# A linear-attention layer and an MLP on one core, issued in an order that a list scheduler in the kernel works out

## The chip, the core and the metric

The kernel runs on one core of one Trainium2 chip. The core has five engines with an instruction queue each: PE (TensorE, matrix products), DVE (VectorE), ACT (ScalarE, also activation functions), POOL (GpSimd) and SP (SyncE, here only for DMAs). Each queue is worked off in its order; engines wait for each other through semaphores. Operands lie in SBUF, 128 partitions wide; PE writes to PSUM, which has eight banks of 512 fp32 columns. 16 DMA engines move data between HBM and SBUF, or within SBUF. The metric is the device time of one execution in microseconds (us), lower is better. A change of about 1% is what a measurement of this kernel can tell from none.

## What is computed

Attention over 8 batches, 8 heads, 576 tokens and head size 64 without a softmax, followed by an MLP on all 4608 tokens (512 → 2048 → 512) with h·cos(h) between its layers.

```python
def phi(x, c, s):
    r = np.maximum(x, 0.0)
    return np.concatenate([r * c, r * s], axis=-1)
q_p, k_p = phi(q, cos_w, sin_w), phi(k, cos_w, sin_w)    # by token: cos, sin of (pi/2) * pos / S
kv = np.einsum('bhsf,bhsd->bhfd', k_p, v)
z = np.sum(k_p, axis=2)
num = np.einsum('bhsf,bhfd->bhsd', q_p, kv)
den = np.einsum('bhsf,bhf->bhs', q_p, z)[..., None] + 1e-06
x = (num / den).transpose(0, 2, 1, 3).reshape(B * S, H * D)
h = x @ w_in
out = (h * np.cos(h)) @ w_out
```

## The kernel before

**Tiles.** A batch's 576 tokens are laid on 128 partitions in four full tiles of 128 tokens (t = 0 to 3) and half a tile (t = 4, 64 tokens). Two batches, an even and an odd one, use opposite halves of the partitions of t = 4, so that the half tiles of a pair make one full tile. All matrix operands are fp16, loads and outputs fp32.

**Stages of one batch.** `load` (L79) brings k, v and q into one raw buffer each (two DMAs on SP per tensor). `prep` (L89) computes relu(x)·cos and relu(x)·sin for a token tile: with `tensor_scalar` on DVE (L98), and in batch 0 the sine half on ACT (L96). `prep_v` (L102) casts v into the 65 columns of V1 (the last one is ones, for the denominator). `kv_group` (L111) makes 20 products of 65 columns for four heads (L117) and ACT copies the result into kvz (L120). `q_trans` (L123) transposes a tile of q, eight heads, on PE through an identity (L127) and ACT copies it to qT (L131). `num` (L136) makes eight products of 65 columns (L147; 16 for t = 4 of an odd batch), and DVE computes the denominator (L152), its reciprocal (L155) and x16 (L159). `x_trans` (L164) transposes x16 in four pieces on PE (L168), ACT copies it to xT (L176).

**Stages of the MLP.** `moe1` (L225) makes one bank of layer 1, four products of 512 columns (L230), and `gate` (L220) follows: the sine of h + pi/2 on ACT into ch (L222), the product with h on DVE into g (L223). 16 banks make a chunk, which is one batch's 512 main tokens. `moe1_rem` (L235) does the same for the 128 remaining tokens of a pair of batches, 64 products of 128 columns (L242). `moe2` (L257) makes 128 output rows with 16 products of 512 columns (L260); ACT copies them (L270, L280), SP stores them.

**Order.** `mlp(s)` (L285) lists the steps of layer 1 of batch s with the layer 2 of batch s − 1 spread in between; `attention(b)` (L178) lists the attention's steps; `spread` (L303) mixes the MLP of s with the attention of s + 1. The framework orders the engines' queues from there and sets all waits. PSUM is a pool of eight tiles of one bank each, given out in turn. Weights are loaded and cast to fp16 by DMAs on POOL: w_in (L330) after a small copy (L325) that waits for q of batch 0, w_out (L338) after one (L333) that waits for v of batch 1. The loads of batch 1 wait, through copies at L84, for the third quarter of w_in.

Of the kernel before, what the change touches and what calls it, by code (L numbers as in the profile page):

```python
# [13 lines left out]
F16 = mybir.dt.float16  # L14


@with_exitstack
def kernel(
# [21 lines left out]
    assert Dm == H * D and R == P // 2 and 2 * D == P  # L40


# [6 lines left out]
    for n in range(2):  # L49
# [7 lines left out]
    cpool = ctx.enter_context(tc.tile_pool(name="cpool", bufs=1))  # L57
    apool = ctx.enter_context(tc.tile_pool(name="apool", bufs=2))
    gpool = ctx.enter_context(tc.tile_pool(name="gpool", bufs=2))
    ppool = ctx.enter_context(  # L60
        tc.tile_pool(name="ppool", bufs=8, space=bass.MemoryType.PSUM))

    CS = cpool.tile([P, 2, 2, NT + 1], F32, name="CS")
    IDENT = cpool.tile([P, P], F16, name="IDENT")
    PIH = cpool.tile([P, 1], F32, name="PIH")
    w_in_sb = cpool.tile([P, NCT, Dff], F16, name="w_in_sb")
    w_out_sb = cpool.tile([P, NJT, Dm], F16, name="w_out_sb")
    V1 = [cpool.tile([P, NT + 1, H, D1], F16, name=f"V1_{n}") for n in range(2)]

    srcs = {"k": k, "v": v, "q": q}  # L70
    raw = {nm: cpool.tile([P, H, NT + 1, D], F32, name=f"{nm}m") for nm in srcs}
    kvzs, kps, qps, qts, xts, gts = {}, {}, {}, {}, {}, {}

    def tokens(ap, n):

        return (ap[..., 0:S5, :].rearrange("h (p t) d -> p h t d", t=NT + 1),
                ap[..., S5:S, :].rearrange("h (p t) d -> p h t d", t=NT))

    def load(b, name, after=None):  # L79
        if b >= B:  # L80
            return
        m, n = raw[name], b % 2
        if after is not None:
            nc.gpsimd.tensor_copy(out=m[0:2, 0, 0, 0:1], in_=after)  # L84
        five, four = tokens(srcs[name][b], n)
        nc.sync.dma_start(out=blocks(m, n), in_=five)
        nc.sync.dma_start(out=blocks(m, 1 - n)[:, :, 0:NT, :], in_=four)

    def prep(b, name, dst, t):  # L89


        in_ = raw[name][:, :, t, :]
        for g in range(2):
            sc = CS[:, b % 2, g, t:t + 1]
            if b == 0 and g == 1:
                nc.scalar.activation(out=dst[:, t, :, g, :], in_=in_, func=AF.Relu, scale=sc)  # L96
            else:
                nc.vector.tensor_scalar(  # L98
                    out=dst[:, t, :, g, :], in0=in_, scalar1=0.0, scalar2=sc,
                    op0=ALU.max, op1=ALU.mult)  # L100

    def prep_v(b):  # L102
        vt = raw["v"].rearrange("p h t d -> p t h d")
        for n, (t0, t1) in enumerate(((0, 2), (2, NT + 1)) if b == 0 else ((0, NT + 1),)):
            dst = V1[b % 2][:, t0:t1, :, 0:D]
            if b == 0 and n == 0:
                nc.scalar.activation(out=dst, in_=vt[:, t0:t1], func=AF.Copy)
            else:
                nc.vector.tensor_copy(out=dst, in_=vt[:, t0:t1])  # L109

    def kv_group(b, hb):  # L111
        kp, kvz = kps[b], kvzs[b]
        KV = ppool.tile([P, HB, D1], F32, name=f"KV{b}_{hb}", tag="ps")
        for hh in range(HB):
            h = hb * HB + hh
            for t in range(NT + 1):
                nc.tensor.matmul(  # L117
                    KV[:, hh, :], lhsT=kp[:, t, h].rearrange("p g d -> p (g d)"),
                    rhs=V1[b % 2][:, t, h, :], start=(t == 0), stop=(t == NT))
        nc.scalar.activation(  # L120
            out=kvz[:, hb * HB:(hb + 1) * HB, :], in_=KV, func=AF.Copy)

    def q_trans(b, t):  # L123
        src = qps[b][:, t]
        QP = ppool.tile([P, H, P], F16, name=f"QP{b}_{t}", tag="ps")
        for h in range(H):
            nc.tensor.matmul(  # L127
                QP[:, h, :], lhsT=src[:, h].rearrange("p g d -> p (g d)"),
                rhs=IDENT, is_transpose=True)
        qT = apool.tile([P, H, P], F16, name=f"qT{b}_{t}", tag=f"qT{t}")  # L130
        nc.scalar.activation(out=qT, in_=QP, func=AF.Copy)  # L131
        qts[(b, t)] = qT

    x16s = {}

    def num(b, t):  # L136

        parts = [(qts[(b, t)], kvzs[b])]
        if t == NT:
            parts.insert(0, (qts[(b - 1, t)], kvzs[b - 1]))  # L140
        N = [ppool.tile([P, HB, D1], F32, name=f"NUM{b}_{t}_{hb}", tag="ps")
             for hb in range(2)]
        for hb in range(2):
            for hh in range(HB):
                h = hb * HB + hh
                for n, (qT, kvz) in enumerate(parts):
                    nc.tensor.matmul(  # L147
                        N[hb][:, hh, :], lhsT=qT[:, h, :], rhs=kvz[:, h, :],
                        start=(n == 0), stop=(n == len(parts) - 1))
        den = apool.tile([P, H], F32, name=f"den{b}_{t}", tag="den")  # L150
        for hb in range(2):
            nc.vector.tensor_scalar_add(  # L152
                out=den[:, hb * HB:(hb + 1) * HB], in0=N[hb][:, :, D], scalar1=1e-6)
        rec = apool.tile([P, H], F32, name=f"rec{b}_{t}", tag="rec")
        nc.vector.reciprocal(out=rec, in_=den)  # L155
        x16 = apool.tile([P, H, D], F16, name=f"x16{b}_{t}", tag="x16", bufs=4)
        for hb in range(2):
            sl = slice(hb * HB, (hb + 1) * HB)
            nc.vector.tensor_tensor(  # L159
                out=x16[:, sl, :], in0=N[hb][:, :, 0:D],  # L160
                in1=rec[:, sl].unsqueeze(2).broadcast_to((P, HB, D)), op=ALU.mult)
        x16s[(b, t)] = x16

    def x_trans(b, t):  # L164
        x2 = x16s.pop((b, t)).rearrange("p h d -> p (h d)")
        XP = ppool.tile([P, NCT, P], F16, name=f"XP{b}_{t}", tag="ps")
        for c in range(NCT):
            nc.tensor.matmul(  # L168
                XP[:, c, :], lhsT=x2[:, c * P:(c + 1) * P], rhs=IDENT,
                is_transpose=True)  # L170
        if t < NT:
            dst = xts[b][:, :, t * P:(t + 1) * P]
        else:
            dst = xts[("r", b // 2)] = apool.tile(
                [P, NCT, P], F16, name=f"xTr{b}", tag="xTr")
        nc.scalar.activation(out=dst, in_=XP, func=AF.Copy)  # L176

    def attention(b, after=None):  # L178

        kps[b] = apool.tile([P, NT + 1, H, 2, D], F16, name=f"kp{b}", tag="kp", bufs=1)  # L180
        qps[b] = apool.tile([P, NT + 1, H, 2, D], F16, name=f"qp{b}", tag="qp", bufs=1)
        kvzs[b] = apool.tile([P, H, D1], F16, name=f"kvz{b}", tag="kvz", bufs=3)
        xts[b] = apool.tile([P, NCT, SM], F16, name=f"xT{b}", tag="xT")

        def pk(t):
            return lambda: prep(b, "k", kps[b], t)

        def pq(t):
            return lambda: prep(b, "q", qps[b], t)

        def ld(name):
            return lambda: load(b + 1, name, after)

        def of(f, t):
            return lambda: f(b, t)

        def pv():
            prep_v(b)
        if b == 0:
            steps = [pk(t) for t in range(NT + 1)] + [ld("k"), pq(0)]  # L200
            for t in range(1, NT + 1):
                steps += [of(q_trans, t - 1), pq(t)]
            steps += [ld("q"), of(q_trans, NT), pv, ld("v"), of(kv_group, 0),
                      of(kv_group, 1), of(num, 0)]
        else:
            steps = [pk(t) for t in range(NT + 1)] + [ld("k"), pv, ld("v")]
            steps += [of(kv_group, 0), pq(0), of(kv_group, 1), pq(1)]
            for t in range(2, NT + 1):
                steps += [of(q_trans, t - 2), pq(t)]
            steps += [ld("q"), of(q_trans, NT - 1), of(num, 0), of(q_trans, NT)]  # L210
        steps += [
                  of(num, 1), of(num, 2), of(x_trans, 0), of(num, 3),
                  of(x_trans, 1)]
        if b % 2 == 1:
            steps += [of(num, NT), of(x_trans, 2), of(x_trans, 3), of(x_trans, NT)]
        else:
            steps += [of(x_trans, 2), of(x_trans, 3)]
        return steps

    def gate(dst, M1, n):  # L220
        ch = apool.tile([P, SM], F32, name="ch", tag="ch", bufs=3)
        nc.scalar.activation(out=ch[:, 0:n], in_=M1, func=AF.Sin, bias=PIH, scale=1.0)  # L222
# [62 lines left out]
    def mlp(s):  # L285
# [8 lines left out]
        if not m1:  # L294
            return m2
# [76 lines left out]
```

## Time and profile before

| | |
|---|---|
| Median of three runs | 348.44 us (346.4 to 349.01) |
| The profiled execution's span | 347.7 us |
| PE / DVE / ACT busy | 308.7 / 213.2 / 185.9 us |
| HBM read, written | 36.74 MB, 9.44 MB |
| First layer-1 matmul | 30.65 us |
| Last matmul starts a group of 16 at | 339.24 us |
| k, q, v of batch 0: from first DMA issue to use | 0.74 to 7.15, 10.72, 14.08 us |
| Mean of one: gate on ACT, gate on DVE, prep on DVE, prep on ACT | 0.69, 0.69, 0.48, 0.63 us |
| Copy of a q transpose (1024), an x transpose (512), an output (512), all on ACT | 1.00, 0.60, 0.60 us |

How to read it: the page gives busy time by engine, then the span in 40 equal slices (each digit is the busy share in tenths, PEclk is the clock that TensorE was granted), the DMA queues, the chain of work that ended last, and the costliest groups of instructions. A group is named by line, engine, operation, and output <- inputs. The trace can also be asked for a timeline. Matmuls are pipelined: the duration of one in the profile includes its way through the array, so the pace is read from the starts.

### The profile page before, as it was taken

Reading aid. Unit: us, or ns where it says so; the run is one execution under the profiler, and the core shown is the slowest. Engines: PE = TensorE matmul, PEld = TensorE weight load, DVE = VectorE, ACT = ScalarE, POOL = GpSimd, SP = SyncE. Lnnn points to the kernel's source line nnn. Section 1 sums busy time; section 2 is a strip of 40 time slices with the busy share of each in tenths; the row PEclk is TensorE's granted clock in tenths of the full one; section 3 lists DMA queues with packets and bytes.
Section 4 is the critical chain, followed back from the end, with each engine's and each line's share of the span. In section 5 each row is a group of like instructions: output and inputs, shape, how many; then the busy total and the mean of one; then the engine's idle time right before and its main releaser. Section 6 shows DMA issues by size and latency. Waiting matters only on the chain.

```text
span 347.7 us, 6066 instructions
## 1 busy us (share of the span) xinstructions
PE 308.7 (89%) x2448; PEld 172.2 (50%) x2448; DVE 213.2 (61%) x486; ACT 185.9 (53%) x285; POOL 8.4 (2%) x19
## 2 busy tenths in 40 slices
PE   0555099599999999999999999999999999999994
PEld 0442066245565555455574555455655554446441
DVE  3536949978698499239983897356953481444100
ACT  1954048356755575356664665557555753555211
POOL 0400400000000000000000000000000000000000
PEclk9986679789999999999999999999999999999998
DMA  7999999226536464411833134301010010110121
GB/s 237 281 229 314 209 223 340 63 92 211 161 100 200 146 189 163 136 63 38 265 100 130 39 129 125 134 2 63 1 62 30 2 61 1 60 61 1 62 91 61
DMA packets 33084, 42.38 MB, mean 122 GB/s; under 512 B 1824, under 2 KB 30496, under 8 KB 33056
## 3 DMA queue, kind: packets, MB, share of 16 engines
q1 hardware_dynamic: 28544, 37.75, 32.9%
q0 software_dynamic: 4224, 4.19, 7.4%
q8 instruction: 19, 0.31, 0.4%
q14 instruction: 9, 0.07, 0.1%
q10 hardware_dynamic: 288, 0.04, 0.1%
HBM read 36.74 MB, written 9.44 MB: 133 GB/s over the span
## 4 chain that ended last, share of the span: by engine, by line
PE 81%; DVE 4%; issue 4%; ACT 3%; DMA 2%; POOL 0%; POOLq 0%; DVEq 0%
DMA km<-in_k_dram 2%; ACT ch L222 2%; DVE qp_332 L98 1%; PE M_4083 L260 1%; PE M_4044 L260 1%; PE M_3984 L260 1%; PE M_3876 L260 1%; PE M_3816 L260 1%; PE M_3757 L260 1%; PE M_3696 L260 1%; PE M_3421 L260 1%; PE M_2682 L260 1%; PE M_2424 L260 1%; PE M_2064 L260 1%; PE M_1780 L260 1%
## 5 line engine op out<-in xcount | busy, mean ns | idle before, releaser
L230 PEld LDWEIGHTS <-w_in_sb 128*128 128x128 f16 x512 | 48.0, 101 | 47.4 <-issue 7.4
L242 PEld LDWEIGHTS <-w_in_sb 128*128 128x128 f16 x256 | 14.8, 98 | 0.2
L127 PE MATMUL QP_0_115<-IDENT,qp_97 128*128 128x128 f16 x8 | 1.0, 311 | 12.9 <-ACT qp_97 L96 12.9
L109 DVE CAST V_1_73<-vm 128x2560 f16<-128x2560 f32 x4 | 11.3, 2814 | 0.0
L109 DVE CAST V_0_72<-vm 128x2560 f16<-128x2560 f32 (+1 forms) x4 | 10.2, 2539 | 1.4 <-DMA vm<-in_v_dram 1.4
L127 PEld LDWEIGHTS <-qp_97 128*128 128x128 f16 x40 | 4.2, 149 | 12.9 <-ACT qp_97 L96 12.9
L260 PEld LDWEIGHTS <-g_3716 128*128 128x128 f16 x64 | 6.3, 98 | 7.5
L260 PEld LDWEIGHTS <-g_3243 128*128 128x128 f16 x64 | 6.2, 98 | 7.3
L260 PEld LDWEIGHTS <-g_727 128*128 128x128 f16 x64 | 6.2, 98 | 7.1
L260 PEld LDWEIGHTS <-g_2729 128*128 128x128 f16 x64 | 6.2, 98 | 7.1
L260 PEld LDWEIGHTS <-g_1728 128*128 128x128 f16 x64 | 6.1, 97 | 7.1
L260 PEld LDWEIGHTS <-g_341 128*128 128x128 f16 x64 | 6.2, 98 | 7.1
L260 PEld LDWEIGHTS <-g_2242 128*128 128x128 f16 x64 | 6.1, 98 | 7.1
L260 PEld LDWEIGHTS <-g_1241 128*128 128x128 f16 x64 | 6.1, 98 | 7.1
L117 PE MATMUL KV_0_375<-V_1_73,kp_331 128*128 128x65 f16 x20 | 1.3, 243 | 8.7 <-DVE V_1_73 L109 8.7
L117 PEld LDWEIGHTS <-kp_331 128*128 128x128 f16 x40 | 2.5, 132 | 9.7 <-issue 9.5
L98 DVE TENSOR_SCALAR kp_331<-km,CS 128x512 f16<-128x512 f32 x10 | 4.2, 480 | 2.7 <-DMA km<-in_k_dram 2.7
L120 ACT ACTIVATE kvz_333<-KV_0_375 128x260 f16<-128x260 f32 x1 | 0.4, 388 | 9.3 <-PE KV_0_375 L117 9.3
L96 ACT ACT_TABLE_LOAD x1 | 1.3, 1283 | 7.1 <-DMA km<-in_k_dram 7.1
L98 DVE TENSOR_SCALAR kp_96<-km,CS 128x512 f16<-128x512 f32 x5 | 2.1, 480 | 4.7 <-DMA km<-in_k_dram 4.7
L223 DVE TENSOR_TENSOR g_3716<-M_3717,ch 128x512 f16<-128x512 f32 x1 | 0.7, 691 | 6.9 <-ACT ch L222 6.9
L223 DVE TENSOR_TENSOR g_1728<-M_1729,ch 128x512 f16<-128x512 f32 x1 | 0.7, 693 | 6.6 <-ACT ch L222 6.6
(1072 smaller groups left out, 841.4 us busy)
## 6 DMA issues: line engine op xcount, KB each, us to landing
out_dram<-ost SPq DMA_DIRECT2D x32, 256.0 KB, 2.4
km<-in_k_dram SPq DMA_DIRECT2D x8, 640.0 KB, 5.3
qm<-in_q_dram SPq DMA_DIRECT2D x8, 640.0 KB, 6.0
vm<-in_v_dram SPq DMA_DIRECT2D x8, 640.0 KB, 7.0
km<-in_k_dram SPq DMA_DIRECT2D x8, 512.0 KB, 4.9
qm<-in_q_dram SPq DMA_DIRECT2D x8, 512.0 KB, 4.8
vm<-in_v_dram SPq DMA_DIRECT2D x8, 512.0 KB, 7.3
w_in_sb<-in_moe_w_in_dram POOLq DMA_DIRECT2D x4, 512.0 KB, 9.1
```

The source lines that it names most:

```text
L96: nc.scalar.activation(out=dst[:, t, :, g, :], in_=in_, func=AF.Relu, scale=sc)
L98: nc.vector.tensor_scalar(out=dst[:, t, :, g, :], in0=in_, scalar1=0.0, scalar2=sc, op0=ALU.max, op1=ALU.mult)
L109: nc.vector.tensor_copy(out=dst, in_=vt[:, t0:t1])
L117: nc.tensor.matmul(KV[:, hh, :], lhsT=kp[:, t, h].rearrange("p g d -> p (g d)"), rhs=V1[b % 2][:, t, h, :], start=(t == 0), stop=(t == NT))
L120: nc.scalar.activation(out=kvz[:, hb * HB:(hb + 1) * HB, :], in_=KV, func=AF.Copy)
L127: nc.tensor.matmul(QP[:, h, :], lhsT=src[:, h].rearrange("p g d -> p (g d)"), rhs=IDENT, is_transpose=True)
L222: nc.scalar.activation(out=ch[:, 0:n], in_=M1, func=AF.Sin, bias=PIH, scale=1.0)
L223: nc.vector.tensor_tensor(out=dst, in0=M1, in1=ch[:, 0:n], op=ALU.mult)
L230: nc.tensor.matmul(M1, lhsT=w_in_sb[:, c, j * P:(j + 1) * P], rhs=xts[b][:, c, :], start=(c == 0), stop=(c == NCT - 1))
L242: nc.tensor.matmul(M1[:, jj, :], lhsT=w_in_sb[:, c, j * P:(j + 1) * P], rhs=xts[("r", pr)][:, c, :], start=(c == 0), stop=(c == NCT - 1))
L260: nc.tensor.matmul(M2, lhsT=gts[key][:, j, gsl], rhs=w_out_sb[:, j, :], start=(j == 0), stop=(j == NJT - 1))
```

## The change

The whole function is rewritten; what each stage computes stays. What differs:

- A class `Plan` collects steps, each with an engine, an assumed occupancy and latency, a due time, and what it reads and writes. `run` is a list scheduler: it gives each engine in turn the ready step that can start first, the earlier due time first, and returns all steps by their start. The steps are then issued in this order, and the framework's own ordering is off (`manual_schedule`); it still sets the waits.
- All buffers are allocated once. PSUM is four tiles of two banks: two for layer 1, one for layer 2, one (ATT) for attention.
- The remainders of the eight batches (8 x 64 = 512 tokens) are gathered in xR and run as a ninth chunk, after batch 7.
- Layer 1 of chunks 0 and 1 runs by token halves: two products groups of 256 columns fill a bank.
- From batch 2 on, q tiles and x tiles are transposed by DMAs on SP, within SBUF; the batch 1 remainder's x too. Batch 0 leaves out t = 4 of q until layer 1 has begun (`late_q0`).
- The cosine half of every prep is on DVE, the sine half on ACT (batch 0's t = 4 of q apart, both on DVE). V is cast by token tile, in batches 0 and 1 by head halves and on both engines.
- num's denominator and x16 are one DVE instruction each for all heads, not two.
- w_in waits for the first half of v of batch 0, w_out for the second quarter of w_in, the loads of batch 1 (but for v's second half) for the third quarter of w_out.
- ACT's sine table is loaded at the start by a tiny activation. The last output tile is copied in two halves, on ACT and DVE, and stored from two queues.

```diff
+class Plan:
+    LINK = {"PE": 0.12, "ACT": 0.05, "DVE": 0.05, "POOL": 0.1, "SP": 0.0}
...
+        while len(order) < len(st):
+            best = None
+            for e, cand in ready.items():
+                for n in cand:
+                    t = max(free[e], avail[n])
+                    key = (t, st[n]["due"], n)
+                    if best is None or key < best[0]:
+                        best = (key, e, n)
+            (t, _, _), e, n = best
...
+        return [st[n] for n in sorted(order, key=lambda n: (st[n]["start"], n))]
...
-    ppool = ctx.enter_context(
-        tc.tile_pool(name="ppool", bufs=8, space=bass.MemoryType.PSUM))
+    M1P = [ppool.tile([P, 2, SM], F32, name=f"M1_{n}") for n in range(2)]
+    M2P = ppool.tile([P, 2, Dm], F32, name="M2")
+    ATT = ppool.tile([P, 2, SM], F32, name="ATT")
+    M1 = [M1P[n // 2][:, n % 2, :] for n in range(4)]
+    M2 = [M2P[:, n, :] for n in range(2)]
...
+    MM, MMH, MMA, MMT = 0.2157, 0.109, 0.031, 0.057
+    T0, TW, TP = 17.0, 46.0, 30.0
+    start = [T0, TW] + [TW + 14.0 + TP * n for n in range(NC)]
...
+    def q_dma(b, t, due):
+        dst, dkey = qdst(b, t)
+        pl.add("SP", 0.62, 0, due, lambda: nc.sync.dma_start(
+            out=dst, in_=qp[:, t].rearrange("p h g d -> p (h g d)"), transpose=True),
+            [("qp", t, g, h) for g in range(2) for h in range(H)], [dkey],
+            dma=(262.0, 200.0))
...
+    def x_dma(b, t, n, due):
+        dst, dkey = xdst(b, t)
+        pl.add("SP", 0.62, 0, due, lambda: nc.sync.dma_start(
+            out=dst, in_=x16[n].rearrange("p h d -> p (h d)"), transpose=True),
+            [("x16", n)], [dkey], dma=(131.0, 200.0))
...
+    def gate(bank, key, dst, dkeys, due):
+        c = chn[0] % NCH
+        chn[0] += 1
+        act(0.59, due, lambda: nc.scalar.activation(
+            out=ch[c], in_=bank, func=AF.Sin, bias=PIH, scale=1.0), [key, "PIH"], [("ch", c)])
+        dve(0.61, due, lambda: nc.vector.tensor_tensor(
...
+    def layer1(c):
+        X = xT[c % 2] if c < B else xR
...
+        for j in range(NJT):
+            m = m1n[0] % 4
+            m1n[0] += 1
+            due = start[c] + j * width[c] / NJT
+            def mm(m=m, j=j):
+                for cc in range(NCT):
+                    nc.tensor.matmul(M1[m], lhsT=w_in_sb[:, cc, j * P:(j + 1) * P], rhs=X[:, cc, :],
+                                     start=(cc == 0), stop=(cc == NCT - 1))
+            pe(NCT, MM, due, mm, xk + [("w_in", j // 4)], [("M1", m)])
+            gate(M1[m], ("M1", m), G[:, j, :], [("g", c % 2, j, t) for t in range(NT)], due + 1.5)
...
+    def attention(b):
+        T = start[b]
...
+        early = b == 1
+        base = T - 37.0
+        for nm in "kqv":
+            if early:
+                hold_raw(nm, 2)
+            load(b, nm, base - 12, HALVES if early and nm == "v" else (slice(0, H),))
+        for t in range(NT + 1):
+            for g in range(2):
+                prep(b, "k", t, g, "DVE" if g == 0 else "ACT", base + 1.5 * t)
...
+            if early:
+                q_pe(b, t, *BANKS[t % 4], "ACT" if t % 2 else "DVE", tt + 1)
+            else:
+                q_dma(b, t, tt + 1)
...
+    with tc.manual_schedule():
+        setup()
+        for s in pl.run():
+            s["fn"]()
```

## The prediction

> **What bounds the kernel now.** I read the page's head and slices first, then the timeline of TensorE (PE) over the first 70 us, then a dense stretch.
>
> ```profile
> span 347.7 us, 6066 instructions
> PE 308.7 (89%) x2448; PEld 172.2 (50%) x2448; DVE 213.2 (61%) x486; ACT 185.9 (53%) x285; POOL 8.4 (2%) x19
> ...
> PE   0555099599999999999999999999999999999994
> ...
> PEclk9986679789999999999999999999999999999998
> DMA  7999999226536464411833134301010010110121
> ```
>
> PE is full from slice 8 on, and full of holes before (a slice is 8.7 us). The timeline shows the holes; its columns are start, length, engine, line, operation, count, and the idle time before with what ended it:
>
> ```profile
> 30.65 1.86 PE L230 MATMUL M_342<-xT_99,w_in_sb 128*128 128x512 f16 x4 [0.69 <-ACT xT_99 L176]
> 32.31 1.91 PE L230 MATMUL M_354<-xT_99,w_in_sb 128*128 128x512 f16 x4
> 34.02 1.49 PE L230 MATMUL M_365<-xT_99,w_in_sb 128*128 128x512 f16 x4
> 44.20 1.26 PE L117 MATMUL KV_0_375<-V_1_73,kp_331 128*128 128x65 f16 x20 [8.70 <-DVE V_1_73 L109]
> ...
> 66.74 0.40 PE L168 MATMUL XP_4_688<-IDENT,x_4_665 128*128 128x128 f16 x2 [3.77 <-DVE x_4_665 L159]
> ```
>
> The first layer 1 starts at 30.65, stops after three banks, and PE waits 8.7 us for batch 1's cast. From starts in dense stretches PE pushes a 512-column matmul in 0.216 us, 128 columns in 0.057, 65 columns in 0.031. Before: 512+576 of the first (234.7), 256+320+144 = 720 of the second (41.0), 640 of the third (19.8): 295.5 us of work. The last matmul is pushed at 342.7 (339.24 + 16 x 0.216). Up to 68.8 it had pushed 23.7 us of work (80 QP, 80 KV, 80 NUM, 36 XP, 56 layer-1 matmuls), so **45 us are lost before 68.8**; after it 273.9 us hold 271.8 of work. PE's work plus the start is the time; DVE and ACT are idle 40% and more, and 5.0 us follow the last push.
>
> [...] three groups from 30.65 take 1.71 us each instead of 0.86, PEclk 0.5 to 0.8. [...]
>
> **The change, part by part.**
>
> *PE's work.* 240 q transposes and 112 x transposes leave PE (352 x 0.057 = **−20.1**). Layer 1 keeps its columns: four remainders of 128 columns become a ninth chunk of 512, chunks 0 and 1 run 256 columns wide (0.108 each). After: 448+576 x 0.2157 + 256 x 0.108 + 112 x 0.057 + 640 x 0.031 = **274.7 us**.
>
> *Start.* The w_in hold on POOL moves from q to v's first half, so k, q and v (landed at 7.1, 10.7, 14.0) no longer share the wires with it until about 12.5; its first quarter then lands about 16 to 17, not late for layer 1. I follow the built order: ACT's sine table is loaded early (1.28 us out of the way); kp and qp to about 13; four transposes to 14.2; their copies (1.0 each, alternately DVE and ACT, on two-bank tiles) to 16.8, V's casts in between; KV's second half waits for ACT's copy of the first, 18.0; NUM about 19.3 to 20.2; x16 on DVE (0.15+0.2+0.75) 21.0 and 22.1; two xT copies by 23.4; layer 1 at **23.8** instead of 30.65, with 4.7 us of work pushed: 19.1 lost. Cold clock on it, as at 30.65 before: 2.5.
>
> *Batch 1.* w_out now loads during layer 1 of chunk 0, where before w_out waited for v of batch 1 (36.3); k, q and half of v of batch 1 are held for w_out's third quarter. 15.5 MB in all, at the 300 to 390 GB/s of the loads before, land by about 50; layer 2 of chunk 0 (13.8 us of work) covers that. At chunk 1's start NUM, x16, transpose and copy follow each other with little in between: three x16 in a row (0.75 each), two copies of 0.6, a fourth NUM and its chain: about **6** lost. Queued behind these waits are kp and qp of batch 2 on ACT and DVE, which wait for loads themselves; they gate xT's last copies, but at 62 to 66 us, about when PE gets there.
>
> *A new wait.* PSUM is now four tiles of two banks each, and the built order shows that the waits are by tile, not by bank. Where layer 1 runs alone, PE writes both banks; sine 1 waits for both, product 1 for it, sine 2 for product 1, product 2 for sine 2, and PE's next write into either bank for product 2. Durations:
>
> ```profile
> 149.90 1.03 PE L230 MATMUL M_1770<-xT_1236,w_in_sb 128*128 128x512 f16 x4
> 150.96 0.69 ACT L222 ACTIVATE ch<-M_1770,PIH 128x512 f32<-128x512 f32 x1 [0.18 <-PE M_1770 L230]
> 151.68 0.69 DVE L223 TENSOR_TENSOR g_1728<-M_1770,ch 128x512 f16<-128x512 f32 x1 [0.17 <-ACT ch L222]
> ```
>
> The group is pushed by 150.76, the sine starts 0.20 later. Chain: 0.20 + 4 x 0.69 + 4 hops (0.03 to 0.05) = 3.1 us, and 1.73 of writing: 4.83 us for every two pairs of banks, in which PE has 3.45 us to do. **1.4 lost for each four banks after the first four.** Chunks 0, 1 and 2 run all 16 banks so (3 x 1.4 each), chunk 3 about 13, chunk 4 about 10: 12.6 + 3 + 2.1 = about 18. Other instructions in the DVE and ACT queues between (preps 0.48 and 0.63, V's casts) add about 3.
>
> From there layer 1 and layer 2 alternate. There the second bank's write waits for sine 1: 0.20 + 0.69 + 0.05 = 0.94 against 0.86 of layer 2 in between, 35 x 0.08 = 2.8. Layer 2's two banks wait for each other's copy: 0.20 + 0.60 + 0.05 = 0.85 against 0.86, nothing while ACT is free; if it isn't, up to 0.6 each. NUM waits for DVE's x16 through one tile ATT, 1.5 us against 1.7 to 2 of cover: 3 in all. Preps in ACT's and DVE's queues: 3.
>
> *Work moved between DVE and ACT.* ACT gets about 70 preps (x 0.63) and loses 30 qT copies (1.0) and 28 xT copies (0.6); DVE loses the preps. Both stay near 60% busy: nothing, as long as the orders hold.
>
> *SP.* 30 q transposes (262 KB) and 28 x transposes (131 KB) go into SP's in-order queue, before later loads and stores. Per batch: 5 of the first, 4.5 of the second, 10 other DMAs at 0.63. [...] hidden, since each transpose stands some 10 us or more of PE work ahead of its reader. Bounds: at a load's rate 0.8 us; if the queue is held until landing, like the nearest rows (2.4 to 6.0 us), some 5 us. [...] Nothing on PE waits then.
>
> *Tail.* The last output is copied in two halves and sent from two queues: 4.3 instead of 5.0 us.
>
> **Sum:** 274.7 + 19.1 + 2.5 + 6 + 18 + 3 + 2.8 + 3 + 3 + 4.3 = 336.4 against the span of 347.7; the median of the runs is 0.7 above that span, so **337**.
>
> **Rivals.**
> - *The pair waits cost little* (0.17): sine, sine, product, product stands in places, which shortens the chain to 2.9 us, and idle time of DVE and ACT speaks for it. Without most of the 30 us of waits: about 316.
> - *SP becomes the bound* (0.20), slower than before: a q transpose that holds SP for 5 us makes a batch 25 + 11.3 + 6.3 = 42.6 us against a chunk's 33, over six batches +58: about 395. It decides from 3.7 us per q transpose ((33 − 6.3) / 7.25); at 4.2 it equals the time before. For it: every transpose stands before loads in one queue, and nothing here has measured one. Against: the later slices show DMA mostly at 0 to 4 tenths[...].
> - *The queues pile up* (0.13): loads of batches 2 and 3 stand in ACT's and DVE's order before work that PE waits for; each late load of 3 to 5 us stops all. Three or four of these: about 352.
> - *The fixed order doesn't do what it says*, PE keeps its holes: then the start stays at 45 lost, less 20 of work, plus the waits: in the pile-up case.
>
> **How the numbers follow.** The forecast's case has 0.50 and its own range is 322 to 346. Within 1% (345.0 to 351.9, about what a measurement of this kernel can tell from no change) lie a few hundredths of it and about half of the pile-up. Faster: 0.44 + 0.17 = 0.61; same 0.12; slower, from the SP case and the rest of the pile-up, 0.27. The range 317 to 372 leaves out about half of the first rival and most of the SP case's upper part.
>
> **What would show it.** Right: first layer-1 matmul near 24 us; in chunks 0 to 2 PE idle before each second pair, ended by DVE's product, about 1.1 and 0.3 us in turn; few waits on DMA transposes; PE pushing 274.7 us of work[...]. Wrong: PE waiting for xT or qT from SP, issues of 4 us and more, or PE near full from 24 us on.

## The result and the profile after

| | before | after |
|---|---|---|
| Median of four runs | 347.42 us (346.25 to 349.01) | 352.28 us (350.4 to 353.1) |
| The profiled execution's span | 347.7 us | 348.6 us (time 350.4) |
| First layer-1 matmul | 30.65 us | 23.59 us |
| PE's work by the pace of starts | 295.6 us | 274.7 us |
| Time PE lost from then to its last push | 22 us, to 342.7 us | 50 us, to 343.8 us |

In the trace of before a matmul of 512 columns lasts 379 ns and the next starts 216 ns after it, one of 128 columns lasts 219 ns at a pace of 57, one of 65 columns 193 ns at a pace of 31.

The ratio is 1.0125, 95% interval 1.0076 to 1.0175: the change made the kernel slower by 1.25%. The forecast was 337 us and faster. A single execution below, of the version with refitted times, took 867.75 us, as PE pushed most of its 512-column matmuls in 0.62 us in place of 0.216, and the ratio there leaves it out. The head and slices of the changed kernel's page:

```profile
span 348.6 us, 5319 instructions
...
PE 292.8 (84%) x2032; PEld 154.1 (44%) x2032; DVE 181.0 (52%) x387; ACT 179.2 (51%) x290; POOL 7.9 (2%) x19
...
PE   0478899676888779878988998999999999999983
...
PEclk9989999999999999999999999999999999999998
DMA  6999958999999989798494641561041010101111
```

PE begins earlier and has 20 us less to do, and all of it is lost again in sixes, sevens and eights that reach to slice 25, at an almost full clock (0.99 on average) and with DVE and ACT at 52% and 51%. The chain of work that ended last says who holds PE: 57% of it is PE, 19% ACT, 12% DVE. The view of PE's waits (who waited for whom: us in total, times, longest):

```profile
PE M L436 <- ACT ost L448: 10.9, 20, 0.9
PE M L412 <- DVE gT L370: 9.0, 14, 1.3
PE M L395 <- DVE gT L370: 6.5, 7, 2.0
```

L412 and L395 are layer 1, waiting for the gate's product. L436 is layer 2, waiting for the copy of a bank by ACT. The second and third were forecast as a loss; the first was named in the prediction and put at nothing. How they come about is seen in the timeline. In chunk 2, where layer 1 runs alone (start, length, engine, line, operation, count, idle before):

```profile
113.06 1.89 PE L412 MATMUL M<-xT,w_in_sb 128*128 128x512 f16 x8 [1.28 <-DVE gT L370]
...
113.64 0.69 ACT L368 ACTIVATE ch<-M,PIH 128x512 f32<-128x512 f32 x1 [0.78 <-DVE gT L370]
114.35 0.69 DVE L370 TENSOR_TENSOR gT<-M,ch 128x512 f16<-128x512 f32 x1 [0.75 <-ACT ch L368]
115.04 0.69 ACT L368 ACTIVATE ch<-M,PIH 128x512 f32<-128x512 f32 x1 [0.72 <-PE M L412]
115.10 1.89 PE L412 MATMUL M<-xT,w_in_sb 128*128 128x512 f16 x8 [0.16 <-DVE gT L370]
...
115.76 0.69 DVE L370 TENSOR_TENSOR gT<-M,ch 128x512 f16<-128x512 f32 x1 [0.71 <-ACT ch L368]
116.48 1.29 ACT L368 ACTIVATE ch<-M,PIH 128x512 f32<-128x512 f32 x2 [0.76 <-DVE gT L370]
```

Sine, product, sine, product follow each other without overlap, 0.70 us apart; PE writes the next pair (115.10) when the earlier pair's second product is over, and the one after that at 117.95. That is 4.89 us for four banks (113.06 to 117.95), as worked out in the prediction (4.83), for 3.45 us of work.

The tail of the program has layer 2 alone. PE, and what ACT does at the same time:

```profile
332.62 3.61 PE L436 MATMUL M<-w_out_sb,gT 128*128 128x512 f16 x16 [0.69 <-ACT ost L448]
336.92 3.61 PE L436 MATMUL M<-w_out_sb,gT 128*128 128x512 f16 x16 [0.69 <-ACT ost L448]
341.22 2.75 PE L436 MATMUL M<-w_out_sb,gT 128*128 128x512 f16 x12 [0.69 <-ACT ost L448]
```

```profile
331.98 0.60 ACT L448 ACTIVATE ost<-M 128x512 f32<-128x512 f32 x1 [3.70 <-PE M L436]
336.27 0.60 ACT L448 ACTIVATE ost<-M 128x512 f32<-128x512 f32 x1 [3.70 <-PE M L436]
```

ACT has been idle for 3.70 us, so the copy is as early as it can be; still PE, which goes on to the *other* bank, begins only when the copy is done. From 332.62 to 336.92 are 4.30 us, in which PE has 16 x 0.2157 = 3.45 us of work: **0.85 us lost per bank**, although ACT is free. In the kernel before, where each bank is a tile, the same stretch has no such gap: PE starts a bank every 3.45 us, and the copy of the bank before runs beside it.

```profile
332.34 3.62 PE L260 MATMUL M_4044<-w_out_sb,g_3716 128*128 128x512 f16 x16
332.54 0.60 ACT L270 ACTIVATE ost<-M_4025 128x512 f32<-128x512 f32 x1 [2.86 <-PE M_4025 L260]
335.79 3.62 PE L260 MATMUL M_4064<-w_out_sb,g_3716 128*128 128x512 f16 x16
```

Where layers 1 and 2 alternate, the copy stands behind a sine that the pair of layer 1 had delayed:

```profile
243.31 0.69 ACT L368 ACTIVATE ch<-M,PIH 128x512 f32<-128x512 f32 x1 [1.91 <-DVE gT L370]
243.90 0.59 ACT L448 ACTIVATE ost<-M 128x512 f32<-128x512 f32 x1
```

and PE's next write to layer 2's tile stands at 244.54, after an idle 0.50 us (it started the group before at 243.18 and pushed it in 0.86).

Adding up, over the whole trace, each matmul's start less the start and the push of the one before gives this comparison with the terms of the prediction's sum:

| Term | predicted | after |
|---|---|---|
| PE's work | 274.7 | 274.7 |
| Lost before the first layer-1 matmul | 19.1 | 18.9 |
| Cold clock on layer 1 | 2.5 | 0 |
| Chunk 1's start (42.9 to 67.7 us) | 6 | 4.2 |
| Layer 1 alone, pair waits and queued work | 18 + 3 | 22.9 |
| Layer 2's waits for copies | **0** | **14.3** |
| Alternation, num, preps | 2.8 + 3 + 3 | 8.5 |
| Tail | 4.3 | 4.8 |
| Span | 336.4 | 348.3 (348.6 in the trace) |

The 14.3 are 8.5 between one bank of layer 2 and the next (10 x 0.85) and 5.8 where layer 2 follows layer 1 (12 times).

### The profile page after: what moved, and what is told of

Same layout as the page of the kernel before. It is cut to its first block, busy times and chain, and to the rows that moved or that the text cites. A ratio compares the mean times of both kernels' runs of the same rounds, so it can differ in the third digit from the quotient of the medians.

```text
span 348.6 us, 5319 instructions
## 1 busy us (share of the span) xinstructions
PE 292.8 (84%) x2032; PEld 154.1 (44%) x2032; DVE 181.0 (52%) x387; ACT 179.2 (51%) x290; POOL 7.9 (2%) x19
## 3 DMA queue, kind: packets, MB, share of 16 engines
q1 hardware_dynamic: 75520, 49.17, 53.3%
## 4 chain that ended last, share of the span: by engine, by line
PE 57%; ACT 19%; DVE 12%; issue 6%; DMA 4%; SPq 0%; DVEq 0%; ACTq 0%
PE M L436 28%; PE M L412 20%; ACT ch L368 10%; DVE gT L370 10%; PE M L395 5%; DMA qm<-in_q_dram 4%; ACT ost L448 4%; ACT qp L233 2%; PE ATT L257 2%; PE ATT L319 1%; DVE x L329 1%; ACT V L246 1%; PE M L288 1%; ACT kp L233 1%; ACT qT L292 0%
## 5 line engine op out<-in xcount | busy, mean ns | idle before, releaser
L370 DVE TENSOR_TENSOR gT<-M,ch 128x512 f16<-128x512 f32 x144 | 98.2, 690 | 110.1 <-ACT ch L368 53.9
L368 ACT ACTIVATE ch<-M,PIH 128x512 f32<-128x512 f32 x144 | 96.6, 686 | 112.5 <-DVE gT L370 83.3
L436 PE MATMUL M<-w_out_sb,gT 128*128 128x512 f16 x576 | 141.0, 379 | 11.4 <-ACT ost L448 10.9
L412 PE MATMUL M<-xT,w_in_sb 128*128 128x512 f16 x384 | 94.7, 378 | 11.7 <-DVE gT L370 9.0
L436 PEld LDWEIGHTS <-gT 128*128 128x128 f16 x576 | 54.6, 97 | 76.7 <-issue 18.1
L412 PEld LDWEIGHTS <-w_in_sb 128*128 128x128 f16 x448 | 43.2, 97 | 68.2 <-issue 21.1
L395 PE MATMUL M<-xT,w_in_sb 128*128 128x256 f16 x256 | 30.4, 272 | 8.3 <-DVE gT L370 6.5
L448 ACT ACTIVATE ost<-M 128x512 f32<-128x512 f32 x35 | 20.6, 592 | 32.1 <-PE M L436 32.1
L395 PEld LDWEIGHTS <-w_in_sb 128*128 128x128 f16 x256 | 24.6, 97 | 13.1 <-issue 6.8
L233 ACT ACTIVATE kp<-km,CS 128x512 f16<-128x512 f32 x40 | 26.2, 712 | 4.9 <-DMA km<-in_k_dram 4.9
L233 ACT ACTIVATE qp<-qm,CS 128x512 f16<-128x512 f32 x39 | 26.2, 713 | 2.7 <-DMA qm<-in_q_dram 2.7
L329 DVE TENSOR_TENSOR x<-ATT,rec 128x512 f16<-128x512 f32 x30 | 20.6, 688 | 0.6
L412 PE MATMUL M<-xR,w_in_sb 128*128 128x512 f16 x64 | 16.4, 379 | 0.0
```

The lines of the kernel that those rows point to most:

```text
L233: act(0.2 + 0.37 * f, due, lambda: nc.scalar.activation(out=out_, in_=in_, func=AF.Relu, scale=sc), rd, wr)
L329: dve(0.62, due, lambda: nc.vector.tensor_tensor(out=x16[n].rearrange("p (b h) d -> p b h d", b=2), in0=N[:, :, :, 0:D], in1=rec[n].rearra ...
L368: act(0.59, due, lambda: nc.scalar.activation(out=ch[c], in_=bank, func=AF.Sin, bias=PIH, scale=1.0), [key, "PIH"], [("ch", c)])
L370: dve(0.61, due, lambda: nc.vector.tensor_tensor(out=dst, in0=bank if len(dst.shape) == 2 else bank.rearrange("p (j s) -> p j s", j=dst.sh ...
L395: nc.tensor.matmul(M1[m][:, jj * 2 * P:(jj + 1) * 2 * P], lhsT=w_in_sb[:, cc, j * P:(j + 1) * P], rhs=X[:, cc, ts], start=(cc == 0), stop= ...
L412: nc.tensor.matmul(M1[m], lhsT=w_in_sb[:, cc, j * P:(j + 1) * P], rhs=X[:, cc, :], start=(cc == 0), stop=(cc == NCT - 1))
```

## Experiments

Theory A: the waits go by PSUM tile, not by bank, so engines that use different banks of one tile follow each other in program order, in layer 1 and in layer 2. Theory B: the DMA transposes hold PE up, through late xT and qT or by their traffic. Theory C: the order that the list scheduler fixes is at fault, in whatever tiles. The kernel before ran beside all of them, 347.3 to 347.5 us; ratios are to it.

### Layer 1's and layer 2's banks as tiles of their own

The built order of steps is the same in the changed kernel and in these three; only the tiles differ. Batches 0 and 1 use the same banks for num, so there the denominator and x16 are made in two instructions of four heads where the tile is split.

```diff
-    M1P = [ppool.tile([P, 2, SM], F32, name=f"M1_{n}") for n in range(2)]
-    M2P = ppool.tile([P, 2, Dm], F32, name="M2")
-    M1 = [M1P[n // 2][:, n % 2, :] for n in range(4)]
-    M2 = [M2P[:, n, :] for n in range(2)]
+    M1 = [ppool.tile([P, SM], F32, name=f"M1_{n}") for n in range(4)]
+    M1P = [(M1[0], M1[1]), (M1[2], M1[3])]
+    M2 = [ppool.tile([P, Dm], F32, name=f"M2_{n}") for n in range(2)]
+    M2P = tuple(M2)
```

Layer 1's part alone:

> Layer 1's four PSUM banks are four tiles of one bank; layer 2's tile and ATT stay as they are, and so does the order of the instructions. Theory A (waits go by tile, so PE waits for the products of both banks of a pair): the 23 us of waits in the stretches of layer 1 alone and some 3 us where layer 1 meets layer 2 go: about 326 us (321 to 333); the 0.85 us waits for layer 2's copies stay. Theory B (the DMA transposes hold PE through late xT and qT, or by their traffic): no change, 349 to 353. Theory C (the fixed order of the list scheduler is the cause, in whatever tiles): 345 to 353.

Measured: **318.31 us** (317.15 to 319.66), ratio 0.9158 (0.9116 to 0.92). Layer 2's part alone:

> Layer 2's two banks are two tiles; layer 1 stays in pairs. Theory A: the waits of PE for layer 2's copies go, ten of 0.85 us in the stretches of layer 2 alone and up to 5 us where layer 2 follows layer 1: about 341 us (337 to 346). Theories B and C: no change, 349 to 353.

Measured: **339.15 us** (338.35 to 340.9), ratio 0.9773 (0.9735 to 0.981). Both:

> Layer 1's and layer 2's banks all are tiles of their own, only ATT keeps two banks. Theory A: both savings add up, about 317 us (312 to 324), PE full from about 24 us on as it was in the kernel before from 69 us on. If the DMAs become the bound once PE runs faster (their share is near one until 165 us): 325 to 335, with PE waiting for xT, qT or late loads. Theories B and C alone: 345 to 353.

Measured: **313.08 us** (312.29 to 314.3), ratio 0.9018 (0.8989 to 0.9047). PE's waits with layer 1 split:

```profile
PE M L458 <- ACT ost L470: 7.6, 12, 0.7
PE M L370 <- DVE x L347: 1.9, 4, 1.1
```

With layer 2 split:

```profile
PE M L434 <- DVE gT L392: 9.0, 14, 1.3
PE M L417 <- DVE gT L392: 5.8, 7, 1.4
PE M L434 <- ACT ch L390: 3.7, 5, 1.3
```

And PE's row of slices with both split:

```profile
PE   0479999699999999699999999999999999999994
```

Lines have moved: L434 and L417 are layer 1, L458 layer 2, L470 its copy. Each split takes away its own wait and leaves the other: the waits for the gate's product are gone from the first list and whole in the second, the waits for the copy the other way round. The first saved 34.0 us of the 352.28, more than the 26 expected. A part of layer 2's waits went with it: in its trace exactly ten gaps of 0.85 us between banks of layer 2 are left, and those after layer 1 are down from 5.8 us in all to a single one of 0.4, since the sine ahead of the copy is no longer late. The second saved 13.1. Together they save 39.2, less than 34.0 + 13.1, for the same reason. (By the profiled spans, 348.6, 317.5, 336.7 and 310.5, the savings are 31.1, 11.9 and 38.1.) Theories B and C foresaw no change. They are out as causes of the lost 40 us: the order and the DMA transposes are the same in all three.

### One tile of four banks

```diff
-    M1P = [ppool.tile([P, 2, SM], F32, name=f"M1_{n}") for n in range(2)]
+    M1A = ppool.tile([P, 4, SM], F32, name="M1")
+    M1P = [M1A[:, 2 * n:2 * n + 2, :] for n in range(2)]
```

> Layer 1's four banks are one tile, the order unchanged: the suspected wait is made worse. Theory A: each bank's matmuls, sine and product follow each other, about 0.86 + 0.2 + 0.69 + 0.69 + 0.1 = 2.5 us a bank, 41 us for 16 banks of a chunk, where PE has 14 to do; against about 18 to 19 now in the stretches of layer 1 alone that is some 20 us for each of the first three chunks, and 1 to 1.7 us for each of the 96 banks from there on that layer 2 covers only in part: 420 us, at least 390. Theories B and C: 349 to 356.

Measured: **532.4 us** (531.4 to 532.91). The direction is theory A's, the size is not: the estimate was 112 us too low. The clock had no place in the estimate. The row of granted clock:

```profile
PEclk9999999975559955598558956999999999999999
```

In this trace a bank where layer 1 runs alone takes 2.59 us while the clock is full (from 243.92 to 246.51 us), near the 2.5 of the estimate, and 3.44 us where it is half (195.16 to 198.60). But the three other executions had a lower mean clock, 0.816 against 0.863, and took no longer, so how much of the 112 us the clock accounts for stays open.

### The transposes back on PE

The DMA transposes are undone, once in the split version and once in the changed kernel with its pairs; the scheduler then works out a new order around them.

```diff
-            if early:
-                q_pe(b, t, *BANKS[t % 4], "ACT" if t % 2 else "DVE", tt + 1)
-            else:
-                q_dma(b, t, tt + 1)
+            q_pe(b, t, *BANKS[t % 4], "ACT" if t % 2 else "DVE", tt + 1)
...
-                x_dma(b, t, n, tt + 1)
+                x_pe(b, t, n, ATT[:, 0, :], ("ATT", 0), "ACT", tt + 1)
```

> As the one with both split, but the q and x transposes from batch 2 on are on PE again, 352 matmuls of 0.057 us = 20 us of work, with copies on DVE and ACT. Theory A with the transposes' DMAs harmless: both split plus about 20, 335 to 342 us. If the DMA transposes hold PE up in the version with both split: less than 10 above it, or below it. Theory B alone: clearly faster than the changed kernel, 330, and than the version with both split.

> The changed kernel, its tiles in pairs, with the q and x transposes from batch 2 on back on PE. Theory A (waits by tile): 20 us of transposes come back to PE; a part of them falls into waits that are there anyway, five q transposes of 0.46 us for each batch into the stretches of layer 1, so 358 to 372 us. Theory B (the DMA transposes hold PE up): below 350.

Measured: **332.75 us** (332.23 to 333.28) in the split version, 19.7 above it: the 20.1 us of work, with PE's gaps about the same in sum (19.5 us against 19.0). In the changed kernel with pairs **398.81 us** (396.9 to 400.35), 46.5 above it, where 6 to 20 were expected. So theory B is wrong in sign as well, and the expectation that transposes would fall into the idle time was wrong too. In the pairs' version the group of layer 1 now waits about twice as long as before (columns: busy us, mean ns, then idle time before it and what ended most of it):

```profile
L412 PE MATMUL M<-xT,w_in_sb 128*128 128x512 f16 x384 | 90.7, 378 | 22.3 <-DVE gT L370 20.1
```

That the q transposes, which use layer 1's banks there and are read by a copy of 0.69 us on DVE or 1.02 on ACT, join the same chain by pairs is the likely reason. It was not tried by itself. What is shown is that the DMA transposes, with the order that goes with them, gained 46.5 us under pairs and 20 without.

### Pairs in the kernel before

The part done alone: layer 1 of the kernel before takes its banks from two tiles of two banks; all other uses share four tiles of one bank. The control gives layer 1 four tiles of one bank.

```diff
-        tc.tile_pool(name="ppool", bufs=8, space=bass.MemoryType.PSUM))
+        tc.tile_pool(name="ppool", bufs=4, space=bass.MemoryType.PSUM))
...
+    def bank(i):
+        if i % 2 == 0:
+            pair[0] = ppool.tile([P, 2, SM], F32, name="M1", tag="m1", bufs=2)
+        return pair[0][:, i % 2, :]
...
-        M1 = ppool.tile([P, SM], F32, name="M1", tag="ps")
+        M1 = bank(j)
```

> The kernel before, with layer 1's banks taken in pairs from a pool of two tiles of two banks; the other uses share four tiles of one bank. Its order puts 3.5 us of layer 2 after every four banks of layer 1 and attention pieces of 0.3 to 0.6 us between banks. Theory A: chunk 0, where layer 1 runs alone, loses 1.4 us for each four banks, and in the rest two banks in a row are mostly followed by others before the 3.1 us of their pair's chain are over: 4 us at the least, up to 1.4 us x 35 = 50 us; about 365 us (352 to 395). Theory C (pairs are harmless under an order made as this one is): 346 to 351.

> The control to the pairs in the kernel before: layer 1 has four tiles of one bank of its own, the other uses share the other four. If the pairs are what costs there, this is near the kernel before, 345 to 352. If it is the division of the pool into four and four, this is as slow as the one with pairs.

Measured: **358.85 us** (358.41 to 359.76) with pairs, ratio 1.0316 (1.0286 to 1.0346), and **342.44 us** (341.73 to 343.36) in the control, ratio 0.985 (0.9822 to 0.9878). The pairs cost 16.4 us, and the division of the pool gained 5 us that no theory had. PE's waits for the gate's product, first with pairs, then in the control:

```profile
PE M L237 <- DVE g L223: 11.4, 23, 1.5
```

```profile
PE M L230 <- DVE g L223: 1.5, 3, 0.7
```

Most of the difference lies not where layer 1 runs alone but in the dense part: after 70 us PE's gaps add up to some 18 us with pairs and 4 in the control. There the layer 2 in between covers only a part of the chain, so an order that alternates the layers doesn't make pairs harmless.

### Token halves, and the scheduler's assumed times

Chunks 0 and 1 at full width, in the split version (the condition for halves is never met):

> Both split, and chunks 0 and 1 run at full width (512 columns) as the other chunks do, so that layer 1 waits for all four tiles of xT. In the version with both split the first layer-1 matmul stands at 22.4 us; the fourth tile's copy would let it start at about 24.3, so 1.7 us are lost at chunk 0 and 1 to 2 at chunk 1: 315 to 317 us. If the halves bring nothing: 312 to 314.

Measured: 314.06 us (313.23 to 314.63), ratio 0.9037 (0.8999 to 0.9075), which cannot be told from the split version's 0.9018. The first layer-1 matmul stands at 25.15 us in place of 22.40, but most of these 2.75 us are not seen in the total. If the halves bring anything, it is about 1 us.

The assumed times set to measured ones, and then batch 3's x transposes on PE:

```diff
-            act(0.2 + 0.37 * f, due, lambda: nc.scalar.activation(
+            act(0.2 + 0.51 * f, due, lambda: nc.scalar.activation(
...
-        act(0.59, due, lambda: nc.scalar.activation(
+        act(0.69, due, lambda: nc.scalar.activation(
...
-                x_dma(b, t, n, tt + 1)
+                if b == 3:
+                    x_pe(b, t, n, ATT[:, 0, :], ("ATT", 0), "ACT", tt + 1)
+                else:
+                    x_dma(b, t, n, tt + 1)
```

> Both split, and the scheduler's assumed times set to the measured ones (preps on ACT 0.71 and on DVE 0.48 us, sine and product 0.69, copies 0.60, x16 0.69, a DMA transpose 1.25 us on SP). The order changes a little. Theory A says that what is left are 19 us of start, some 13 of small waits and the tail; of the 13 the 2.7 us wait for a DMA transpose at 125 us and some of the 5.9 at chunk 1's start may go: 309 to 313 us. If the assumed times don't matter: 312 to 314. If the new order is worse somewhere: 315 and more.

> Both split and refitted times, and batch 3's five x transposes on PE (20 x 0.057 = 1.1 us of work), since in the version with both split PE waited 2.5 us for one of them, which SP had issued late: its DMA transposes there took 1.2 to 3.4 us each to issue. If that wait is still there in the refitted order, 308 to 310.5; if the refitted order has it no more, 311 to 313.

Measured: 310.99 us (median of all four; without the long one 310.72, 309.57 to 311.26), ratio 0.8937 (0.8892 to 0.8982), and **311.18 us** (310.17 to 311.98), ratio 0.8949 (0.8924 to 0.8974). Both beat the kernel before by over 10%. Moving batch 3's transposes makes no difference on top of the refitted times; the refitted version's own trace is of the execution of 867.75 us, so whether the wait that this aimed at was already gone is not shown. In the second's trace PE loses 0.3 us in all after 100 us:

```profile
PE   0389999769999999999999999999999999999994
```

What is left is the start, 5.7 us at chunk 1's start, and the tail. ATT alone still has two banks in a tile; splitting it was not tried.

## Why the prediction was wrong

**The step that failed** is the sentence on layer 2's tile: "Layer 2's two banks wait for each other's copy: 0.20 + 0.60 + 0.05 = 0.85 against 0.86, nothing while ACT is free". The mechanism was seen and its 0.85 us was right to the hundredth. It was set against 0.86 us of layer 1 in between, which exists only while the layers alternate. Chunks 0 to 3 run stretches of layer 2 without layer 1, and so does the tail; at ten changes of bank nothing covers the copy. Even in the alternation ACT was not free: the copy stands behind a sine. Set at 0, it measured 14.3 us in the trace, and splitting that tile alone took 13.1 us away. The sum with 14.3 in place of 0 is 350.7, and the kernel comes out slower than before, as it did. Besides, the median stands 3.7 us above the profiled span of 348.6, where the prediction allowed 0.7.

- **Layer 1's pair waits**: right in mechanism and size, 21 forecast, 22.9 measured, 4.89 us for four banks against 4.83.
- **PE's work, the start, the tail**: right within 0.5 us. The cold clock did not come on layer 1 (2.5 forecast, none seen there: the granted clock is 1.00 from 23.59 to 36 us, where the kernel before had 0.56 from 30.65 to 35.5) and chunk 1's start took 1.8 us less. Alternation, num and preps together were 8.5 against 8.8; how these split among themselves was not tested. That the smaller misses (−2.5, −1.8, −0.3, +1.9, +0.5 us) add up to no more than −2.2 us is luck.
- **ACT and DVE**: both end at about half (51% and 52%), where near 60% was said, and neither is the bound; a prep on ACT takes 0.71 us, not 0.63.
- **SP's transposes**: no wait of PE for a DMA transpose is in the trace, as forecast. How long one holds SP was shown by no run ahead of the prediction, so that they stay hidden was the author's expectation, not a measured sum. What is seen doesn't go by size, as the 7.25 (5 + 4.5 / 2) of the SP rival has it: a q transpose (262 KB) takes 1.26 us to issue and an x transpose (131 KB) 1.23 (medians of 30 and 24), and the longest take 4.07 and 3.45 us. One sum of the SP rival is off: by its own terms it equals the time before at about 3.9 us per q transpose, not 4.2 (348 is 11 us above 337, or 1.83 us for each of six batches: (33 + 1.83 − 6.3) / 7.25).

The rivals: pair waits that cost little are out, since splitting both tiles saves 39 us (that rival's 316 us is close to what the split version takes, 313). SP did not become the bound. The queues did not pile up: with the same order and other tiles no such wait is left. One small case is in the trace, PE's wait of 2.0 us before 74.80, ahead of which DVE had run four preps whose load came 1.2 us late. That rival's "about 352" is the measured median by chance; its mechanism is not what took the time. SP comes next: with both tiles split PE waits for a DMA transpose,

```profile
PE M L434 <- DMA xT<-x: 2.8, 2, 2.5
```

after which it pushes its next eight matmuls in 0.43 us each in place of 0.216. SP's own queue in that trace has a single transpose and a group of three that take longer than 1.2 us each to issue, and the transpose that PE waits for (120.19) stands behind a load of q:

```profile
103.22 3.41 SPq L380 DMA_TRANSPOSE xT<-x  x1
...
109.49 6.43 SPq L298 DMA_TRANSPOSE qT<-qp  x3
116.02 1.24 SPq L380 DMA_TRANSPOSE xT<-x  x1
...
119.43 0.67 SPq L213 DMA_DIRECT2D qm<-in_q_dram  x1
120.19 1.26 SPq L380 DMA_TRANSPOSE xT<-x  x1
```

PE goes on at 127.21, 7.0 us after that issue. What part of the wait is the late issue and what part the slow landing is not separated.

That the order doesn't do what it says is out: PE starts layer 1 where it was worked out, and the same order gives 313 us with other tiles.

## What to carry to other kernels

A buffer that several engines use should be one tile for each piece that is handed over by itself. Here a tile of two banks tied a write to one bank to the reader of the other, and the price was the whole chain of both banks wherever PE had nothing else in between: 4.89 us for four banks of layer 1 in place of 3.45, and 0.85 us for each bank of layer 2. When a wait is said to be covered, name the covering work for every stretch of the program: here "0.85 against 0.86" was true at most where two stages alternate and false wherever one ran alone, and that alone turned the sign. If a rewrite moves little, look for a gain and a new wait of one size: here 20 us less work and an earlier start were paid for with 39 us of waits, which other tiles take away.

## What the runs showed of the hardware

In the changed kernel no wait of PE ends at a DMA transpose; the cost is on the DMA engines. The queue that carries loads, stores and transposes, in the changed kernel and then with the transposes on PE (packets, MB, share of 16 engines' span), each with its count of packets:

```profile
DMA packets 80217, 53.87 MB, mean 155 GB/s; under 512 B 48832, under 2 KB 77760, under 8 KB 80192
...
q1 hardware_dynamic: 75520, 49.17, 53.3%
```

```profile
DMA packets 33307, 42.36 MB, mean 106 GB/s; under 512 B 1920, under 2 KB 30848, under 8 KB 33280
...
q1 hardware_dynamic: 28608, 37.62, 28.3%
```

53.3% of 348.6 us less 28.3% of 398.6 us are 73 us of all 16 engines for 49.17 − 37.62 = 11.55 MB, 158 GB/s while they are at it; the other traffic of that queue moves 37.62 MB in 113 us, 333 GB/s. By this measurement a transposed byte takes about twice the engine time, in packets of which 46,912 more are under 512 bytes. Whether the transposition itself or the small packets cost the time is not separated, and loads that ran slower beside the transposes would be counted in the 73 us too. A q transpose of 262 KB lands 3.5 us after its issue (median of 30).
